# The first batch's token sums of phi as TensorE products with a two-column constant, under a new table of steps

## The chip, the core and the metric

The kernel runs as one launch on one core of a Trainium2 chip. The core's engines are TensorE (matrix products into PSUM), VectorE, ScalarE, GpSimd and SyncE, which here issues the transfers. In the rows they are called PE (with PEld for TensorE's loads of the stationary operand), DVE, ACT, POOL and SP. The metric is the device time of one execution in microseconds (us), taken as the median of a kernel's runs.

## The reference

The inputs are q, k and v of shape 8 x 8 x 576 x 64 (batch, head, token, feature), phi of shape 8 x 8 x 576 x 32, and two weights, 512 x 2048 and 2048 x 512, which arrive as 64-bit floats. The first part is an attention through 32 memories, the second a feed-forward network with a leaky unit.

```
a   = exp(phi - max(phi, axis=tokens))
a   = a / (sum(a, axis=tokens) + 1e-9)
k_m = einsum('bhsm,bhsd->bhmd', a, k)
v_m = einsum('bhsm,bhsd->bhmd', a, v)
scores = (q @ k_m.T) / 8
scores = scores - max(scores)
attn   = exp(scores) / (sum(exp(scores)) + 1e-9)
x = (attn @ v_m), heads side by side           # 4608 x 512
h = x @ w_in                                   # 4608 x 2048
out = maximum(0.01 * h, h) @ w_out             # 4608 x 512
```

The maxima and the sums of phi run over the 576 tokens. Such a sum, for each batch, head and memory, is what the change is about; those over the memories, in the scores' softmax, are not touched.

## The kernel before

**Stages.** The work goes batch by batch. The tokens of all eight heads of a batch are first reduced to the 32 memories: phi lies with 128 rows (two groups g of 64, which is half the heads each) and for each of four heads hh nine slots j of 32 memories (`ld["phi"]`, 128 x 4 x 9 x 32). Step A1 takes maxima over the slots on VectorE (L575), A2 transposes them on TensorE (L589), A3 takes the maximum over rows and builds a diagonal (L596, L599), B0 spreads it back by two products with ones (L605), B1 subtracts and B2 takes the exponential on ScalarE (L614, L620). For the first batch B1 and B2 come in two halves. C1 multiplies the exponentials with k (C10) and v (C11): 72 products of 64 rows, 32 stationary columns and 64 moving columns each, at eight positions of the array (L654), into the two PSUM tiles `pk` of the pool `ps_o`.

**The sums.** B3 adds the exponentials over the nine slots on VectorE (L636 to L639 for the first batch, one reduce at L632 for the others), which leaves sums over slots but not over the 64 rows of each group. C2 transposes these on TensorE into columns 128 to 255 of `pk[0]` (L668), and C30 adds over the 64 rows with a reduce, adds epsilon, takes the reciprocal, and scales it by 1/8 (four operations on VectorE, L677 to L682). C3k and C31 use the reciprocals to form x_k (ScalarE, L689) and x_v (VectorE, L700).

**From there.** D10 and D11 transpose x_k and x_v, D3 and D5 copy the results to SBUF as kT and vT (D6 the low half of vT in later batches). C4, D2 and D4 find a power-of-two scale for the values (L708, L339 and L341, the spread L346, L351). Q0 and Q1 flip the two halves of q on VectorE (L772), E1 computes scores (L793), E2 flips them (L807), and the steps S{chunk}{1 to 8} do the softmax of two chunks: maximum (L827), subtraction (L830), exponential on ScalarE (L835), sum and reciprocal (L839 to L841), scaling (L844), and a flip into the tile `a` (L852 or L857), which is the stationary side of the feed-forward part.

**The weights.** x is never formed: the values of the memories are folded into w_in (W and f steps, products at L909 with vT stationary), so that the first feed-forward product multiplies `a` with the folded weight `w_mem`. The 64-bit weights are loaded in pieces (ld), turned into float32 words by integer operations on ScalarE (L384 and L395) and VectorE (L404; a whole piece is 128 x 768), and later split into a high and a low fp16 half. The first eight units of 96 tokens (u0 to u7; P products at L993, O products at L1061) run in float32, so that they need no split weights; the later ones (p, d and others, L1104 and L1172) in fp16 halves. Bounds on the weights (ci, co, L469 to L487) set the scales of the halves.

**What sets the order.** All of it is cut into named steps, and two strings, `OPENING` and `LATER`, list the steps in the order in which they are emitted. Each engine, and the queue of each engine that issues transfers, runs its own instructions in exactly that order, so the strings are the schedule. `a3.Q0` is step Q0 of batch 3; `z.4` are four idle products of ones with ones, 128 x 512 in float32, which keep TensorE busy (L1260); `f00.1` is the fold of batch 0 with piece 0 of the weight; `p14.2` and `d12.5` are parts of the units 14 and 12.

**Where q is loaded.** The two halves of a batch's q are loaded by SyncE (L566) into the first 12288 bytes of a shared tile `arena`; the tiles of k and v of the same batch (4608 bytes each) lie in part in the same place, so the two transfers of q wait until the products of C10 have read them. The transfer of the next batch's phi (L535) is issued in the same stretch.

## Time and profile before

The median of three runs is 667.87 us (667.07 to 669.79). The profiled execution is another one:

| what | value |
|---|---|
| time of the profiled execution | 668.56 us |
| its span, first to last instruction | 666.0 us |
| TensorE busy | 644.3 us, 97% of the span |
| VectorE busy | 515.2 us, 77% |
| ScalarE busy | 398.6 us, 60% |
| GpSimd busy | 29.8 us, 4% |
| granted TensorE clock, mean over the span | 0.994 of full |
| moved by DMA | 60.37 MB, 91 GB/s in the mean |

A row of a timeline gives the start of an instruction, or of some in a row that are alike, counted from the start of the span, its duration, the engine, the line of the kernel, the operation, the tile written and the tiles read, and their sizes. A bracket at the end is the engine's idle time just ahead of it and what ended that. A float32 product appears as two halves, so `x72` products are 144. A row of the windows gives the busy time of each engine in a stretch, with the granted clock as a share of the full one.

### The profile page before, as it was taken

To read this page: it belongs to the slowest core of one execution; us is meant where nothing else is said; L and a number is where in the kernel's file an instruction comes from. 1 tells how busy PE (TensorE), PEld (TensorE's weight loads), DVE (VectorE), ACT (ScalarE), POOL (GpSimd) and SP (SyncE) were. 2 spreads that over 40 slices of the span, in tenths; PEclk is the share of its full clock that TensorE was granted. 3 is DMA by queue.
4 is the path that set the end of the run, shared out by engine and by line. 5 is a ranking of instruction groups with operands and counts; after the bars stand their busy time and mean duration, and the time that the engine had idled before them with its cause. 6 is when DMAs were issued, how large, how long until landed. Compare 5 with 4: busy or idle time off the path is not lost.

```text
span 666.0 us, 17554 instructions
## 1 busy us (share of the span) xinstructions
PE 644.3 (97%) x7592; PEld 483.1 (73%) x7592; DVE 515.2 (77%) x857; ACT 398.6 (60%) x677; POOL 29.8 (4%) x43
## 2 busy tenths in 40 slices
PE   7799999999999899999998999999999999999997
PEld 3345445665446588888897889898878788989883
DVE  5765869999996699888878885779888887575641
ACT  2789677774663457456644765655665466564543
POOL 0100130000020001000100010000010001000000
PEclk9899999999999899999999999999999999999999
DMA  9989641004602441441051401045103010100101
GB/s 257 400 317 306 239 170 49 1 1 110 188 1 53 103 144 33 109 144 33 10 132 36 142 1 33 5 104 177 33 14 79 15 33 8 27 20 16 33 2 47
DMA packets 32604, 60.37 MB, mean 91 GB/s; under 512 B 4368, under 2 KB 14608, under 8 KB 32528
## 3 DMA queue, kind: packets, MB, share of 16 engines
q1 hardware_dynamic: 32432, 59.13, 29.6%
q8 instruction: 59, 0.97, 0.6%
q10 hardware_dynamic: 96, 0.13, 0.1%
q14 instruction: 17, 0.14, 0.1%
HBM read 49.81 MB, written 9.44 MB: 89 GB/s over the span
## 4 chain that ended last, share of the span: by engine, by line
PE 84%; DMA 8%; DVE 4%; ACT 1%; SPq 1%; issue 1%; DVEq 0%; ACTq 0%
PE po L1172 28%; PE ph L1104 20%; PE po L1061 13%; PE ph L993 8%; PE ph L1172 5%; PE pa L909 4%; DMA arena<-in_q_dram 3%; PE pa L654 2%; PE pa L793 2%; DMA arena<-in_moe_w_in_dram 2%; PE po L1206 1%; DMA wi<-in_v_dram 1%; DMA arena<-in_phi_dram 1%; DMA arena<-in_moe_w_out_dram 1%; DVE arena L772 1%; DVE r1k L575 1%
## 5 line engine op out<-in xcount | busy, mean ns | idle before, releaser
L1172 PEld LDWEIGHTS <-arena 128*128 128x128 f16 x2184 | 209.8, 98 | 32.0 <-issue 9.0
L1120 ACT ACTIVATE wi<-ph,g_sc 128x256 f32<-128x256 f32 (+1 forms) x224 | 99.8, 465 | 167.2 <-PE ph L1104 166.3
L1104 PE MATMUL ph<-a,w_mem 128*128 128x256 f16 (+3 forms) x1440 | 147.1, 247 | 3.3 <-ACT wi L1120 3.1
L1104 PEld LDWEIGHTS <-w_mem 128*128 128x128 f16 x1440 | 115.4, 98 | 18.3 <-issue 6.7
L1172 PE MATMUL po<-wo,arena 128*128 128x256 f16 x936 | 122.5, 273 | 0.0
L1172 PE MATMUL po<-arena 128*128 128x256 f16 x936 | 121.9, 273 | 0.0
L1061 PE MATMUL po<-wo,arena 128*128 128x512 f16 (+1 forms) x384 | 110.7, 434 | 0.0
L1149 DVE TENSOR_TENSOR arena<-arena 128x1024 f16<-128x1024 f32 x52 | 63.2, 1216 | 27.7 <-ACT arena L1145 27.6
L1149 DVE TENSOR_TENSOR arena<-wi,arena 128x768 f16<-128x768 f32 (+1 forms) x60 | 52.9, 882 | 31.5 <-ACT arena L1145 31.3
L1145 ACT CAST arena<-arena 128x1024 f16<-128x1024 f32 x52 | 54.2, 1043 | 10.5 <-DVE arena L1141 10.2
L993 PE MATMUL ph<-a,w_mem 128*128 128x192 f16 (+2 forms) x304 | 53.8, 323 | 1.7 <-DVE a L852 1.7
L1141 DVE TENSOR_TENSOR arena<-wi 128x256 f32<-128x256 f32 x104 | 39.2, 418 | 15.3 <-ACT wi L1120 15.3
L1061 PEld LDWEIGHTS <-arena 128*128 128x128 f16 x288 | 27.8, 98 | 29.3 <-issue 0.9
L1145 ACT CAST arena<-wi 128x768 f16<-128x768 f32 (+1 forms) x60 | 46.5, 775 | 1.8
L1141 DVE TENSOR_TENSOR arena<-wi,arena 128x256 f32<-128x256 f32 x104 | 43.8, 422 | 1.8
L1172 PE MATMUL ph<-wo,arena 128*128 128x256 f16 x312 | 42.6, 273 | 0.0
L876 POOL TENSOR_TENSOR a<-t,a 128x384 f16<-128x384 f32 x22 | 21.4, 997 | 450.9 <-ACT a L871 380.4
L1061 PEld LDWEIGHTS po<-wo,arena 128*128 128x128 f32 x96 | 17.6, 190 | 21.0 <-issue 19.1
L772 DVE STREAM_TRANSPOSE arena<-arena 96x1536 f32<-96x1536 f32 x14 | 24.7, 1766 | 8.0 <-DMA arena<-in_q_dram 3.7
L1000 ACT ACTIVATE arena<-ph,g_sc 128x384 f32<-128x384 f32 x32 | 18.5, 578 | 18.3 <-PE ph L993 17.6
L909 PE MATMUL pa<-wi,vT 64*32 64x512 f16 (+1 forms) x704 | 29.0, 420 | 0.4 <-ACT vT L742 0.4
L993 PEld LDWEIGHTS <-w_mem 128*128 128x128 f16 x240 | 20.8, 98 | 9.3 <-issue 2.7
(204 smaller groups left out, 767.6 us busy)
## 6 DMA issues: line engine op xcount, KB each, us to landing
arena<-in_q_dram SPq DMA_DIRECT2D x16, 576.0 KB, 7.0
out_dram<-obs SPq DMA_DIRECT2D x142, 64.0 KB, 1.7
arena<-in_k_dram SPq DMA_DIRECT2D x28, 288.0 KB, 5.2
arena<-in_v_dram SPq DMA_DIRECT2D x28, 288.0 KB, 5.5
arena<-in_moe_w_in_dram SPq DMA_DIRECT2D x12, 512.0 KB, 7.6
arena<-in_moe_w_out_dram SPq DMA_DIRECT2D x12, 512.0 KB, 6.9
arena<-in_phi_dram SPq DMA_DIRECT2D x7, 576.0 KB, 7.1
arena<-in_moe_w_in_dram SPq DMA_DIRECT2D x8, 256.0 KB, 8.1
```

The source lines that it names most:

```text
L772: nc.vector.transpose(flat, ld["q", g].rearrange("p hh j d -> p (hh j d)"))
L876: nc.gpsimd.tensor_tensor(lo[:, tb], t2[:, tb], hi[:, tb], ALU.subtract)
L909: nc.tensor.matmul(pf[g][cols, :], lhs, rhs, start=(n == 0), stop=(n == len(passes) - 1), tile_position=(g * D, hh * M),)
L993: nc.tensor.matmul(ph[:, t0:t0 + n * SB], lhs, rhs, start=(m == 0), stop=(m == len(seq) - 1))
L1000: nc.scalar.activation(dst, ph, AF.Prelu, scale=sc, alpha=SLOPE)
L1061: nc.tensor.matmul(po, lhs, rhs, start=(f == 0 and m == 0), stop=(f == NQ * NF - 1 and m == len(seq) - 1),)
L1104: nc.tensor.matmul(ph[:, t0:t0 + n], lhs, rhs, start=(m == 0), stop=(m == len(seq) - 1))
L1120: nc.scalar.activation(dst, ph, AF.Prelu, scale=g_sc2[:, j:j + 1], alpha=SLOPE)
L1141: nc.vector.tensor_tensor(gt[:, x], y, z, op)
L1145: nc.scalar.copy(dst[:, 0], src)
L1149: nc.vector.tensor_tensor(dst[:, 1], src, dst[:, 0], ALU.subtract)
L1172: nc.tensor.matmul(acc, g[:, x, s, u], rhs, start=(h == 0 and j == 0 and u == 0 and m == 0), stop=(j == NQ - 1 and u == 1 and m == 2), ski ...
```

## The change

**A constant.** A tile `halves_of_rows` of 128 x 2 in float32 has ones in column 0 for the rows 0 to 63 and in column 1 for the rows 64 to 127 (three fills on GpSimd).

**The sums of the first batch.** Its B3 (four operations on VectorE) and C2 (a transpose) are gone. A new step `a0.C1s` makes 36 products instead, one for each slot and head: stationary is the slot of the exponentials, 128 rows x 32 memories, moving is the constant, two columns. They add up in columns 128 and 129 of `pk[0]`, at four positions of the array, and give the sum over tokens for both groups at once. C30 reads these two columns and loses its reduce. The first product with k into `pk[0]` no longer opens that tile, since the sums do. The later batches compute as before.

**The order.** The whole of `OPENING` and `LATER` is written anew, under the same step names. The number of idle products ahead of the first transpose becomes five in three places, later ones move, and in each of the later phases the transfers come in the order q0, q1, phi of the next batch.

The core of the difference (of `LATER` two places, the stretch of batch 5):

```diff
 OPENING = """
-z.4 a0.phi0 a0.phi1 a0.k a0.q0 a0.A10 a0.A11 a0.A2 a0.q1 a0.A3 a0.B0 z.1 a0.B10 a0.B11 a0.B20
-i0.ld0 a0.B21 a0.C10 a0.B3 i0.ld1 a0.C2 z.1 a0.C30 i0.ld2 a0.Q0 a0.C3k a0.v a0.D10 a0.D3 a0.Q1
-a0.E10 i0.y0 a0.E1 z.3 o0.ld0 i0.h0 a0.E20 i0.y1 a0.E21 i0.t0 o0.ld1 i0.h1 a0.S01 i0.y2 i0.h2
-i0.t1 o0.ld2 a0.S02 o1.ld0 i0.t2 a0.S03 a0.C11 a0.E22 i0.b a0.S11 a0.C31 o1.ld1 a0.S12 a0.D11
-a0.S04 a0.D5 a0.S13 f00.1 o1.ld2 o0.y0 a0.S05 f00.2 i1.ld0 a0.S06 o0.y1 a0.C4 u0.P0 o0.h0
...
+a0.phi0 a0.A10 a0.phi1 a0.A11 a0.k z.3 a0.q0 z.1 z.1 a0.A2 a0.q1 i0.ld0 a0.A3 a0.B0 a0.B10
+a0.B11 a0.B20 a0.B21 i0.ld1 a0.v a0.C1s a0.C10 a0.C30 a0.C3k a0.D10 a0.Q0 a0.D3 i0.y0 i0.ld2
+o0.ld0 a0.Q1 a0.E10 o0.ld1 i0.h0 a0.E1 a0.E22 z.2 a0.E21 i0.y1 a0.S11 i0.h1 i0.t1 i0.y2 a0.E20
+i0.h2 i0.t0 o1.ld0 o0.ld2 a0.S12 a0.C11 a0.S01 a0.S02 a0.S03 i1.ld0 a0.C31 a0.D11 i0.t2 i1.ld1
+a0.D5 i0.b f00.1 f00.2 a0.S04 a0.S05 a0.S13 o0.y0 o1.ld2 a0.S06 z.2 a0.C4 o1.ld1 u0.P0 u0.P1
...
 LATER = """
...
+p15.2 d13.3 v15.2 a5.B20 l14.1 d13.4 p15.3 a5.B3 a5.C10 v15.3 c15.0 l15.0 d13.5 a5.q0 s15 a5.C2
+d13.6 p16.0 a5.C30 p16.1 v16.0 a5.q1 d14.0 a5.C31 v16.1 c15.1 d14.1 a5.C4 a5.D11 a5.C3k d14.2
+l15.1 a6.phi p16.2 a5.Q0 a5.D10 v16.2 a5.D2 a5.D3 d14.3 a5.D4 d14.4 a5.Q1 p16.3 a5.D5 d14.5
...
+    halves_of_rows = const.tile([P, 2], F32, name="halves_of_rows")
+    nc.gpsimd.memset(halves_of_rows, 0.0)
+    for g in range(2):
+        nc.gpsimd.memset(halves_of_rows[g * P // 2:(g + 1) * P // 2, g:g + 1], 1.0)
...
-            n = HP * KJ * M
-            t = wi[3][:, n:n + HP * 4 * M].rearrange("p (hh j m) -> p hh j m", hh=HP, j=4)
-            nc.vector.tensor_tensor(t, ph[:, :, 0:4], ph[:, :, 4:8], ALU.add)
-            nc.vector.tensor_tensor(t[:, :, 0:2], t[:, :, 0:2], t[:, :, 2:4], ALU.add)
-            nc.vector.tensor_tensor(s0, t[:, :, 0], t[:, :, 1], ALU.add)
-            nc.vector.tensor_tensor(s0, s0, ph[:, :, 8], ALU.add)
...
-                            start=(j == 0), stop=(j == KJ - 1), tile_position=(g * D, hh * M),
+                            start=(j == 0 and (b > 0 or kinds == (1,) or g > 0)),
+                            stop=(j == KJ - 1), tile_position=(g * D, hh * M),
+                            skip_group_check=(b == 0),
...
+        def sums_of_phi():
+            var["pk"] = [ps_o.tile([P, E], F32, name="po") for g in range(NG)]
+            for j in range(KJ):
+                for hh in range(HP):
+                    nc.tensor.matmul(
+                        var["pk"][0][hh * M:(hh + 1) * M, P:P + NG], ld["phi"][:, hh, j, :],
+                        halves_of_rows, start=(j == 0), stop=(j == KJ - 1),
+                        tile_position=(0, hh * M), skip_group_check=True,
+                    )
...
+                nc.vector.tensor_scalar_add(r, var["pk"][0][:, P:P + NG], EPS)
```

**TensorE, the start of the program.** Here `ones` and `ident` are constants, `r1k` holds the maxima and then the diagonal, `wi` and `wo` hold k and the exponentials. Before:

```order
L1260 MATMUL pa<-ones 128x512 x4
L589 MATMUL pa<-ident,r1k 128x128
L605 MATMUL pa<-r1k,ones 64x128 x2
L1260 MATMUL pa<-ones 128x512
L654 MATMUL po<-wo_90,wi_86 32x64 x2
```

And with the change:

```order
L1276 MATMUL pa<-ones 128x512 x5
L593 MATMUL pa<-ident,r1k 128x128
L609 MATMUL pa<-r1k,ones 64x128 x2
L665 MATMUL po<-halves_of_rows,wi_90 32x2 x36
L653 MATMUL po<-wo_94,wi_90 32x64 x2
```

A fifth idle product stands ahead of the transpose of the maxima, the one behind the spread is gone, and the 36 sums stand ahead of the products with k.

**VectorE, the softmax of the first chunk.** `t` and `tm` are the scores and their maxima, the operations into `wi` from `arena` are the weight's conversion, `x_v` the scaled values. Before:

```order
L772 STREAM_TRANSPOSE wo_89<-arena 96x1536
L807 STREAM_TRANSPOSE t_308<-pa 128x384 x2
L404 SCALAR_TENSOR_TENSOR wi_84<-arena 128x768
L827 TENSOR_REDUCE tm<-t_308 128x24
L404 SCALAR_TENSOR_TENSOR wi_84<-arena 128x768
L830 TENSOR_TENSOR t_308<-t_308,tm 128x768
L404 SCALAR_TENSOR_TENSOR wi_84<-arena 128x512
L807 STREAM_TRANSPOSE t_308<-pa 128x384
L827 TENSOR_REDUCE tm<-t_308 128x12
L700 TENSOR_SCALAR x_v<-po,r_227 128x64 x2
```

With the change:

```order
L788 STREAM_TRANSPOSE wo_93<-arena 96x1536
L823 STREAM_TRANSPOSE t_338<-pa 128x384 x2
L843 TENSOR_REDUCE tm<-t_338 128x12
L408 SCALAR_TENSOR_TENSOR wi_88<-arena 128x768
L823 STREAM_TRANSPOSE t_338<-pa 128x384
L408 SCALAR_TENSOR_TENSOR wi_88<-arena 128x768
L843 TENSOR_REDUCE tm<-t_338 128x24
L846 TENSOR_TENSOR t_338<-t_338,tm 128x768
L716 TENSOR_SCALAR x_v<-po,r_264 128x64 x2
L408 SCALAR_TENSOR_TENSOR wi_88<-arena 128x512
```

The short chunk's flip and maximum, and the piece that was second among the weight's, now stand ahead of the long chunk's maximum and subtraction; the third piece stands behind them.

**SyncE, the transfers between the k and v of batch 5 and those of batch 6.** Before:

```order
L1039 DMA out_dram<-obs 32x512 x16
L535 DMA arena<-in_phi_dram 128x4x288
L566 DMA arena<-in_q_dram 96x4x384 x2
L546 DMA arena<-in_k_dram 128x576
L546 DMA arena<-in_v_dram 128x576
```

With the change:

```order
L1055 DMA out_dram<-obs 32x512 x8
L570 DMA arena<-in_q_dram 96x4x384 x2
L539 DMA arena<-in_phi_dram 128x4x288
L550 DMA arena<-in_k_dram 128x576
L550 DMA arena<-in_v_dram 128x576
```

The two transfers of q, with q0 the first of them, now go ahead of the next batch's phi.

## Rows read from the trace of the kernel before

**Rows 1.** The page's part 1: busy time of each engine, share, instructions.

```profile
PE 644.3 (97%) x7592; PEld 483.1 (73%) x7592; DVE 515.2 (77%) x857; ACT 398.6 (60%) x677; POOL 29.8 (4%) x43
```

**Rows 2.** Timeline of TensorE, 0 to 40 us: start, duration, operation, tiles, count, [idle].

```profile
6.98 0.27 PE L589 MATMUL pa<-ident,r1k 128*128 128x128 f32 x1
...
10.34 0.37 PE L654 MATMUL po<-wo,wi 64*32 64x64 f32 x10 [0.63 <-ACT wi L620]
...
11.78 0.23 PE L654 MATMUL po<-wi,wi 64*32 64x64 f32 x2
...
29.69 2.76 PE L993 MATMUL ph<-a,w_mem 128*128 128x384 f32 x4 [1.73 <-DVE a L852]
```

**Rows 3.** Timeline of TensorE's weight loads, 6 to 7 us.

```profile
6.12 0.19 PEld L1260 LDWEIGHTS pa<-ones 128*128 128x128 f32 x1 [0.36 <-issue]
6.55 0.14 PEld L589 LDWEIGHTS pa<-ident,r1k 128*128 128x128 f32 x1 [0.24 <-issue]
```

**Rows 4.** Timeline of VectorE, 13 to 30 us.

```profile
13.80 0.17 DVE L682 TENSOR_SCALAR r<-r 128x2 f32<-128x2 f32 x1
...
15.57 1.74 DVE L772 STREAM_TRANSPOSE wo<-arena 96x1536 f32<-96x1536 f32 x1
...
19.40 1.05 DVE L807 STREAM_TRANSPOSE t<-pa 128x384 f32<-128x384 f32 x2 [2.09 <-PE pa L793]
...
21.21 0.94 DVE L827 TENSOR_REDUCE tm<-t 128x24 f32<-128x768 f32 x1
22.07 0.95 DVE L404 SCALAR_TENSOR_TENSOR wi<-arena 128x768 uint32<-128x768 uint32 x1
...
26.04 0.95 DVE L839 TENSOR_REDUCE ts__411<-t 128x24 f32<-128x768 f32 x1
...
28.56 0.98 DVE L852 STREAM_TRANSPOSE a<-t 128x768 f32<-128x768 f32 x1
```

**Rows 5.** Timeline of ScalarE, 20 to 25 us.

```profile
20.49 0.93 ACT L384 ACTIVATE arena<-arena 128x768 uint32<-128x768 uint16 x1
...
23.92 0.84 ACT L835 ACTIVATE t<-t 128x768 f32<-128x768 f32 x1 [1.38 <-DVE t L830]
```

**Rows 6.** Windows: stretch, us, busy PE, PEld, DVE, ACT, POOL, granted clock, DMA, GB/s.

```profile
29.84:33.25 3.41, 3.41 (x7) 1.96 (x8) 2.42 (x8) 2.40 (x5) 1.38 (x1) 0.50 1.03 407
224.40:227.81 3.41, 2.85 (x15) 1.84 (x14) 2.88 (x11) 1.63 (x3) 0.00 (x0) 0.50 0.00 0
100.00:200.00 100.00, 100.00 (x911) 56.16 (x909) 97.15 (x144) 64.21 (x105) 3.94 (x4) 1.00 0.21 58
```

**Rows 7.** Timeline of TensorE, idle marks behind the opening.

```profile
83.62 0.38 PE L487 MATMUL pa<-diag,ones 4*128 4x4 f32 x2 [0.83 <-DVE diag L481]
83.93 2.84 PE L1061 MATMUL po<-wo,arena 128*128 128x512 f32 x6
...
223.46 0.49 PE L346 MATMUL pa<-mdiag,ones 128*128 128x128 f32 x2 [2.15 <-DVE mdiag L341]
...
283.13 0.33 PE L1104 MATMUL ph<-a,w_mem 128*128 128x64 f16 x6 [0.37 <-ACT wi L1120]
...
352.90 0.33 PE L1104 MATMUL ph<-a,arena 128*128 128x128 f16 x3 [1.75 <-ACT wi L1120]
...
521.75 0.81 PE L1104 MATMUL ph<-a,w_mem 128*128 128x256 f16 x6 [1.29 <-ACT wi L1120]
```

**Rows 8.** Timeline of VectorE, flips of q in two of three phases.

```profile
220.88 1.77 DVE L772 STREAM_TRANSPOSE arena<-arena 96x1536 f32<-96x1536 f32 x1 [2.89 <-DMA arena<-in_phi_dram]
...
518.35 1.77 DVE L772 STREAM_TRANSPOSE arena<-arena 96x1536 f32<-96x1536 f32 x1 [1.49 <-DMA arena<-in_q_dram]
```

**Rows 9.** DMA issues of both q, 211 to 214 us: last, us to landing.

```profile
arena<-in_q_dram SPq DMA_DIRECT2D x1, 576.0 KB, 4.9
...
arena<-in_q_dram SPq DMA_DIRECT2D x1, 576.0 KB, 8.4
```

**Rows 10.** The page's part 5: group, count, busy us, mean ns, idle before.

```profile
L1104 PE MATMUL ph<-a,w_mem 128*128 128x256 f16 (+3 forms) x1440 | 147.1, 247 | 3.3 <-ACT wi L1120 3.1
```

## The prediction, made without the result

> **What bounds the kernel now.** I read the engine line of the page first: TensorE is busy for 644.3 of 666.0 us, VectorE for 515.2, ScalarE for 398.6 [rows 1]. So the end is set by the sum of TensorE's work, by the time at which that work starts in earnest, and by every stretch in which TensorE waits. None of the products that make up the bulk is touched by the change; it can win only the 22 us in which TensorE stands, and time at half clock. I then went through TensorE's timeline, row by row, for idle marks.

> They lie in three places. In the opening the first product of the feed-forward part starts at 29.69 us, after 1.73 us of waiting for `a` [rows 2]; from there to 83 us no idle mark follows. In the middle there are a few: 0.83, 2.15, 0.37, 1.75 and 1.29 us are the marks that matter [rows 7]. The rest lies behind the last product, where both orders end alike. [...]

> **The opening.** The chain to 29.69 is: maxima of phi, exponentials, products with k, reciprocal sums, x_k, scores, flips, softmax of chunk 0, L993.

> *The warm-up products.* Before, four stand ahead of the transpose of the maxima (L589), now five. The load of that transpose comes at 6.55 and waited for nothing but the issue [rows 3], and its product starts at 6.98 with no idle mark [rows 2]: the maxima were there, and the warm-ups set its start. A fifth is two more halves, 0.43 us each by the spacing of the last loads (6.12 to 6.55): +0.86 on the chain. The first part of the exponentials then ends not at 10.34 [rows 2] but at 11.2.

> *The sums of phi.* Removed are four adds on VectorE and one transpose (L668); added are 36 float32 products of two columns, ahead of the k products. The trace has no such product. The 72 k products (64 columns, 64 rows) run from 10.34 to 12.01, 23 ns each [rows 2]; by their tile positions eight lie side by side. The new ones fill 128 rows, four side by side, so I take 46 ns: 36 x 46 = 1.66 us. Lower end: 36 x 23 = 0.83 us; nothing at all would change no more, as will be seen. Upper end: the whole-array transpose L589, 0.27 us for its two halves, with nothing side by side: 36 x 0.27 = 9.7 us.

> [...]

> *What the sums gain.* The reciprocal no longer waits for the adds, but the three VectorE operations behind it read the PSUM tile that the k products write too, and in the built program they wait for the last k product. So the sums stand in series with the k products: 11.2 + 1.66 + 1.67 = 14.5, and three operations of 0.20 (0.17 and the gap [rows 4]) give 15.1. Before, the last of the three began at 13.80 and q's second flip ended at 15.57 + 1.74 = 17.31 [rows 4]. The two flips of q (1.74 each, a little of it beside each other) follow directly: 15.1 + 3.4 = 18.5. The second scores wait for that flip, so their end moves from 19.40 [rows 4] by 1.2 to 20.6. The part of the change that gives it its name brings nothing here; the fifth warm-up and the series cost more than the adds did.

> *The softmax of chunk 0.* VectorE has, behind the scores: two flips 1.0, the short maximum 0.5, a weight piece t1, the third flip 0.5, a piece t0, maximum, subtraction. t1 needs ScalarE's second half of piece 1, which ends at 20.49 + 0.93 = 21.42 [rows 5] and hangs on a transfer that is not moved. Long operations follow each other by 0.86 (21.21 to 22.07 [rows 4]). From 22.1: four of them, a flip and the tail of the last: 26.1. The exponential takes 0.84 [rows 5]: 27.0. From there to the end of `a` is 28.56 + 0.98 - 26.04 = 3.5 [rows 4]; 30.5, and the first product at 30.7, +1.0. With the cheap price the chain meets t1 at 21.42 and the product starts at 30.0 (+0.35), also if the sums were free. With the dear one it starts near 38.7 (+9.0). v, asked for one transfer earlier, is no longer awaited in any of these. Late next are the vT copy and the squares, which ScalarE now does behind that exponential.

> *The clock.* Two warm-ups now stand between the fold f00 and the first product, where TensorE idled 1.73 us before the clock fell. I take it that the half-speed stretch at 29.84 goes: 3.41 us, all busy [rows 6], lose 1.7 us of work. Opening in sum: 1.0 - 1.7 = -0.7; ends -1.35 and +7.3. From the first product on, TensorE's queue holds the same work in both orders.

> **The middle.** Of the five waits, three are one mechanism. At 220.88, at 518.35 and once between them (three in all, two shown) VectorE's flip Q0 waits for q, with the spread of the value scale or the activations' halves queued behind it [rows 8]; TensorE's 2.15, 1.75 and 1.29 us follow from them. These are the phases of batches 3, 5 and 7. q can be loaded only after the k and v products have read its place, and in these phases q0 is issued behind q1 (3, 7) or behind the next batch's phi (5). The first of two q transfers lands 4.9 us after its issue, the second 8.4 [rows 9]. In batches 2, 4 and 6 q0 came first, and the wait there is 0.37 [rows 7] or none. The new order asks for q0, q1, phi in every phase. It also has 8 or 9 of TensorE's p and d steps (a p step takes 147.1 us / 224 = 0.65 [rows 10], a d step I set to the same), so 5 to 6 us, between the k products and Q0, and Q0 behind the value scale. So I set the three down to 0.4 each: 5.19 - 1.2 = 4.0. The 0.83 at 83.62 is TensorE waiting for the weight bounds (L481); the new order puts a down product in between, 2.7 us by the one that follows (83.93, to the next step at 86.6) [rows 7]: 0.8. With the 2.15 the second half-speed stretch goes: 2.85 us busy in it [rows 6], 1.4 us.

> Against this I set 1.7 us for new waits: two of the size of the 0.83, since a whole order is replanned and I followed only the phases by hand. From 100 to 200 us VectorE is 97% busy [rows 6], and there the new order puts two long operations more, some 2 us, ahead of the eleventh unit's down products. TensorE has no idle there [rows 6], so there is slack, of a size that no row gives.

> Sum: -0.7 - 4.0 - 0.8 - 1.4 + 1.7 = -5.2 us. The profiled execution took 668.56 us (span 666.0), 0.7 over the median of the runs, 667.87; so 663.4 for that execution and 662.7 for the median.

> **Rivals.**
> *The waits come back elsewhere.* The middle is a new plan, and the order before, planned as a whole too, has 6 us of waits. For it: VectorE's 97%. Against: the named cause, q behind other transfers, is gone in all phases. With all 6 us back and the second half-speed stretch with them, only the opening is left: -0.7, 667.2; with a part, down to 664.5.

> *The opening eats it.* The 36 products at the dear price, +7.3 instead of -0.7: 670.7. For it: four column tiles with a load each for two columns. Against: the k rows.

> *The wait moves from Q0 to Q1 (slower).* Behind Q1 on VectorE stand the low half of vT, which the fold of the next batch needs, and the activations' low halves. Between the k products and that fold stand fourteen p and d steps (9.1 us at 0.65) and small transposes (some 1.0, an estimate): 10.1 us; Q1 and the low half take 2.0. From q1 landing later than 8.1 us, each us is a wait in five phases. The second q took 8.4 with phi close behind [rows 9], which is the 0.4 that I count. At 10.25 us all five stand 2.15: 5 x 2.15 - 6.2 + 1.0 = +5.5, 673; if the clock falls each time as at 223, +1.4 each, 680. Against: in batches 4 and 6, with q0, q1, phi in this order, nothing of the kind shows.

> **How the numbers follow.** Forecast 0.60: 662.7, own range 658.5 to 664.5. Waits elsewhere 0.26: 664.5 to 669. The opening 0.05: 670.7. Q1 0.09: 672 and more. Below 658 only if all waits go and the sums are cheap (-1.35 - 6.0 - 1.4 = 659.1, less the small ones). A range of 658 to 669 leaves out about 2 in 10. A change of 0.5%, 3.3 us, is about what can be told from none: below 664.5 is faster (0.60), to 671.2 the same (0.30), above slower (0.10).

> **What would show it.** Right: the first feed-forward product at 30 to 31 us at full clock; the transpose of the maxima near 7.8; the sums in 0.8 to 1.7 us, and the reciprocal behind the last k product; no wait of Q0 for q; one half-speed stretch less at 224. Wrong: a first product later than 33, idle marks over 1 us in batches 3, 5 or 7, or a new half-speed stretch.

## The result, and the profile after

The changed kernel takes 668.77 us (median of 20 runs, 667.06 to 671.81) where the kernel before, run beside it, takes 667.06 (20 runs, 663.23 to 671.29): a ratio of 1.0032, 95% interval 1.0018 to 1.0046. It is slower, by 0.3%, where 0.8% faster was forecast (662.7 against 667.87). The profiled execution took 671.58 us, 2.8 over its median, with a span of 669.7; that of before took 668.56, 1.5 over its median, with a span of 666.0. So the two executions read here lie 3.0 us apart in time and 3.7 in span, the medians 1.7. The 3.7 us are two large parts of opposite sign.

The page's busy times after [rows 1]: the work on TensorE has hardly grown.

```profile
PE 647.5 (97%) x7663; PEld 486.0 (73%) x7663; DVE 520.9 (78%) x852; ACT 397.7 (59%) x677; POOL 33.3 (5%) x46
```

The timeline of TensorE after, 0 to 42 us (columns as in [rows 2]):

```profile
7.64 0.27 PE L593 MATMUL pa<-ident,r1k 128*128 128x128 f32 x1
...
11.05 0.91 PE L665 MATMUL po<-halves_of_rows,wi 128*32 128x2 f32 x72 [1.73 <-issue]
...
17.96 0.32 PE L653 MATMUL po<-wo,wi 64*32 64x64 f32 x3 [4.11 <-issue]
...
32.34 0.27 PE L653 MATMUL po<-wi,wi 64*32 64x64 f32 x2 [1.56 <-issue]
...
35.70 3.78 PE L1276 MATMUL pa<-ones 128*128 128x512 f32 x4
39.27 2.96 PE L1009 MATMUL ph<-a,w_mem 128*128 128x384 f32 x8
```

The sums are cheap: 72 halves in 0.91 us. But among the products with k, which before ran without a gap, TensorE stands still for 4.11 us, and again for 1.56 among those with v, which stand ahead of the fold. The view names no engine, semaphore or transfer for either ("issue"). The first feed-forward product comes at 39.27 instead of 29.69, so 9.6 us later.

VectorE after, where the reciprocal starts and where `a` is done:

```profile
18.45 0.16 DVE L696 TENSOR_SCALAR r<-po 128x2 f32<-128x2 f32 x1 [7.67 <-PE po L653]
...
35.96 0.98 DVE L868 STREAM_TRANSPOSE a<-t 128x768 f32<-128x768 f32 x1
```

With [rows 4] these divide the 9.6 us. The reciprocal's last step ends at 19.02 instead of 13.97, +5.05, of which 4.11 are the stop. From there to the end of `a` it takes 17.92 instead of 15.57, +2.35. `a` is ready at 36.94, but two idle products, which stand behind the delayed fold, hold TensorE until 39.27: +2.2. The order of VectorE's operations, the stop of 1.56 us ahead of the fold and the clock all bear on the last two parts, and this trace alone doesn't part them. The windows after (columns as in [rows 6]) show two stretches at a granted clock of 0.50 in the opening, where before had the one of 3.41 us; the first begins at 12.40, ahead of the long stop:

```profile
12.40:29.47 17.07, 10.43 (x250) 5.88 (x244) 8.63 (x13) 5.59 (x9) 1.44 (x2) 0.50 1.03 391
32.88:39.71 6.83, 6.37 (x22) 2.25 (x23) 5.27 (x11) 5.23 (x8) 0.00 (x0) 0.50 0.52 182
```

From the first feed-forward product to the end, the kernel before takes 636.3 us (666.0 - 29.69), the changed one 630.4: here it wins 5.9. The windows of the middle after:

```profile
80.00:100.00 20.00, 18.29 (x158) 9.10 (x156) 14.15 (x36) 14.05 (x24) 4.01 (x4) 1.00 0.57 203
100.00:200.00 100.00, 98.26 (x867) 54.40 (x867) 93.22 (x145) 65.59 (x108) 10.09 (x9) 1.00 0.28 82
200.00:300.00 100.00, 99.44 (x1335) 75.34 (x1334) 88.01 (x144) 54.27 (x96) 3.20 (x4) 1.00 0.28 74
300.00:400.00 100.00, 100.00 (x1377) 86.71 (x1375) 90.75 (x144) 61.96 (x108) 4.02 (x5) 1.00 0.29 83
```

TensorE idles 4.5 us from 80 to 600 (0.45 of it between 500 and 600) where the same windows of before add up to 8.1. The waits of 2.15, 1.75 and 1.29 us [rows 7] are gone, and no flip of q waits for a transfer [rows 8]:

```profile
L788 DVE STREAM_TRANSPOSE arena<-arena x14: 1732/1767/1774, 75.2 to 517.6; 96x1536 f32<-96x1536 f32 x14
...
its engine sat idle before it (us, times) until:
  PE pa L653: 1.6, 1
```

In place of the 0.83 at the weight bounds there is a new wait of 1.71, of the scores of batch 1 for kT:

```profile
87.05 1.26 PE L809 MATMUL pa<-arena,kT 32*32 32x192 f32 x57 [1.71 <-ACT kT L752]
```

### The profile page after: what moved, and what is told of

Same layout as the page of the kernel before. It is cut to its first block, busy times and chain, and to the rows that moved or that the text cites. A ratio compares the mean times of both kernels' runs of the same rounds, so it can differ in the third digit from the quotient of the medians.

```text
span 669.7 us, 17690 instructions
## 1 busy us (share of the span) xinstructions
PE 647.5 (97%) x7663; PEld 486.0 (73%) x7663; DVE 520.9 (78%) x852; ACT 397.7 (59%) x677; POOL 33.3 (5%) x46
## 3 DMA queue, kind: packets, MB, share of 16 engines
q1 hardware_dynamic: 32432, 59.13, 29.8%
## 4 chain that ended last, share of the span: by engine, by line
PE 93%; DVE 3%; issue 1%; DMA 1%; ACT 1%; SPq 0%; POOL 0%; ACTq 0%; DVEq 0%; POOLq 0%
PE po L1188 31%; PE ph L1120 21%; PE po L1077 13%; PE ph L1009 7%; PE ph L1188 5%; PE pa L925 4%; PE pa L809 2%; PE pa L653 2%; PE pa L1276 2%; PE po L1222 1%; DMA arena<-in_moe_w_in_dram 1%; PE po L653 1%; DVE wo L423 1%; PE pa L735 1%; PE pa L609 1%
## 5 line engine op out<-in xcount | busy, mean ns | idle before, releaser
L1120 PE MATMUL ph<-a,w_mem 128*128 128x256 f16 (+3 forms) x1440 | 145.5, 246 | 1.0 <-ACT wi L1136 1.0
L1165 DVE TENSOR_TENSOR arena<-arena 128x1024 f16<-128x1024 f32 x52 | 63.8, 1227 | 34.0 <-ACT arena L1161 33.8
L1009 PE MATMUL ph<-a,w_mem 128*128 128x192 f16 (+2 forms) x304 | 52.4, 317 | 0.1
L1077 PEld LDWEIGHTS <-arena 128*128 128x128 f16 x288 | 27.6, 98 | 31.3 <-issue 1.0
L1157 DVE TENSOR_TENSOR arena<-wi,arena 128x256 f32<-128x256 f32 x104 | 47.2, 453 | 1.8
L892 POOL TENSOR_TENSOR a<-t,a 128x384 f16<-128x384 f32 x22 | 23.9, 1109 | 437.9 <-ACT a L887 383.6
L1157 DVE TENSOR_TENSOR arena<-wi 128x256 f32<-128x256 f32 x104 | 40.6, 433 | 0.2
L1016 ACT ACTIVATE arena<-ph,g_sc 128x384 f32<-128x384 f32 x32 | 18.6, 581 | 25.1 <-PE ph L1009 23.8
L954 DVE SCALAR_TENSOR_TENSOR w_mem<-pa,w_mem 128x512 f16<-128x512 f32 x40 | 26.0, 681 | 2.0 <-ACT w_mem L948 1.9
```

Source lines behind the costliest of these rows:

```text
L892: nc.gpsimd.tensor_tensor(lo[:, tb], t2[:, tb], hi[:, tb], ALU.subtract)
L954: nc.vector.scalar_tensor_tensor(t[:, 1], src["w"][g] if b else w32[j][g], ws, t[:, 0], ALU.mult, ALU.subtract)
L1009: nc.tensor.matmul(ph[:, t0:t0 + n * SB], lhs, rhs, start=(m == 0), stop=(m == len(seq) - 1))
L1077: nc.tensor.matmul(po, lhs, rhs, start=(f == 0 and m == 0), stop=(f == NQ * NF - 1 and m == len(seq) - 1),)
L1120: nc.tensor.matmul(ph[:, t0:t0 + n], lhs, rhs, start=(m == 0), stop=(m == len(seq) - 1))
L1157: nc.vector.tensor_tensor(gt[:, x], y, z, op)
```

## What the stops have in common

I counted TensorE's records in the trace from the start of the program: its loads, its products' halves and the semaphore instructions of its sequencer, which the timeline leaves out, together. To one record, the stop of 4.11 us stands in front of the 450th, the one of 1.56 us in front of the 962nd, and a third of 0.85 at 148 us in front of the 2754th: 450, 450 + 2 x 256, 450 + 9 x 256. I call such a place a border. In the kernel before the only stop without a releaser, 0.43 us, is in front of the 450th too, but there that record lies in the scores:

```profile
18.31 0.92 PE L793 MATMUL pa<-wo,kT 32*32 32x192 f32 x38 [0.43 <-issue]
```

The DMA view has a queue of its own for instructions; in the stop, from 15 to 17 us, it shows one packet among the loads (kind, packets, MB, share):

```profile
q1 hardware_dynamic: 277, 0.77, 99.7%
q8 instruction: 1, 0.02, 3.3%
```

That packet starts at 15.56 and ends at 16.61, TensorE goes on at 17.96. The page counts 60 such packets of 0.98 MB in all, so 16 KB each, and the records have 59 borders. So the theory, inferred from these numbers and shown by no view, was: a packet brings the 256 records that follow a border; those behind the 450th record arrive at some 18 us; the 36 sums are 144 records (72 halves and 72 loads), and they moved that border from the scores, which waited for kT and q anyway, into the products with k, on which everything else in the opening waits. The rivals were the new opening order, the clock, and late transfers.

## The experiments

Each ran in five rounds beside the kernel before; e9 and e13, which are not in the table, ran once. "First product" is the first feed-forward product, "stop" the one in front of the 450th record.

| run | median us (runs) | ratio to before, 95% | span of profile | first product | stop |
|---|---|---|---|---|---|
| change | 668.77 (20) | 1.0018 to 1.0046 | 669.7 | 39.27 | 4.11 |
| e1 opening of before | 664.11 (8) | 0.9936 to 0.9972 | 659.8 | 28.45 | under 0.3 |
| e2 later order of before | 675.22 (6) | 1.0102 to 1.0146 | 674.6 | 39.29 | 5.00 |
| e3 before + 36 unused sums | 678.73 (5) | 1.0161 to 1.0208 | 678.1 | 38.04 | 5.04 |
| e4 nine wide sums | 664.79 (12) | 0.9951 to 0.9977 | 662.3 | 33.84 | 0.45 |
| e5 before + 28 unused sums | 676.22 (6) | 1.0107 to 1.0163 | 674.1 | 34.73 | 3.30 |
| e6 e1 + idle products | 663.47 (7) | 0.9918 to 0.9967 | 659.7 | 29.35 | under 0.3 |
| e7 sums on VectorE | 663.87 (8) | 0.9934 to 0.9970 | 661.5 | 31.33 | under 0.3 |
| e8 e4 + idle products | 664.12 (9) | 0.9929 to 0.9966 | 663.3 | 33.27 | 1.43 |
| e10 e7 + idle products | 664.04 (12) | 0.9944 to 0.9977 | 660.5 | 29.82 | under 0.3 |
| e11 change + idle product | 669.63 (12) | 1.0028 to 1.0067 | 667.2 | 37.45 | 5.66 |
| e12 before, q order alone | 663.51 (12) | 0.9939 to 0.9980 | 660.2 | 29.07 | 0.15 |
| e14 idle products cut small | 667.48 (12) | 0.9992 to 1.0025 | 665.7 | 36.76 | 4.70 |
| e15 40 products ahead | 667.75 (12) | 0.9987 to 1.0030 | 665.1 | 36.15 | 3.36 |

### The two halves of the change: e1 and e2

e1 has `OPENING` and the sums of before with the new `LATER`, e2 the reverse:

```diff
 run(OPENING.split())   # e1: of before   e2: of the change
 run(LATER.split())     # e1: of the change   e2: of before
```

> The opening of before (sums on VectorE, a transpose) with the new order behind it. Theory (the loss sits in the opening alone: TensorE gets the instructions behind its 450th record only at some 18 us, and the 36 sums have brought that record into the products with k): first feed-forward product at 29.7 us as before, waits of the middle gone as in the changed kernel; 636.3 us behind that product become 630.4 plus 1.7 for the half-clock stretch at 29.8, so about 663 us (662 to 664) against 667.1 of before. Rival (the middle gains only because it starts 10 us later and its transfers have landed by then): the waits for q come back, 665 to 668.

> The changed opening with the old order behind it. Theory: first feed-forward product near 39 us as in the changed kernel, the middle's waits as before: 667.1 + some 6 = 673 us (671 to 675). Rival (the two parts interact, as above): the old middle has its waits covered by the later start too, 669 to 670.

The loss lies in the opening, the gain behind it: e1 is 0.46% faster than before, e2 1.2% slower. From the first product to the end of the span the new order wins 4.9 us behind either opening (631.4 against 636.3, and 630.4 against 635.3). These are single executions, off their medians by +1.5 (before), -2.0 (e1), +2.8 (the change) and +1.2 us (e2). By the medians the new order wins 2.8 us behind the old opening and 6.5 behind the new one, and both runs come out just above their ranges. Why the two differ is not settled; e2's stop of 5.00 us is longer than the change's, and e2 has a further stop without a releaser of 1.32 us at 451 us.

### The sums put into the kernel before: e3 and e5

```diff
-i0.ld0 a0.B21 a0.C10 a0.B3 i0.ld1 a0.C2 z.1 a0.C30 i0.ld2 a0.Q0 a0.C3k a0.v a0.D10 a0.D3 a0.Q1
+i0.ld0 a0.B21 a0.C1s a0.C10 a0.B3 i0.ld1 a0.C2 z.1 a0.C30 i0.ld2 a0.Q0 a0.C3k a0.v a0.D10 a0.D3 a0.Q1
```

In e5 the added step runs over seven slots instead of nine.

> The kernel before, in its own order, with the 36 two-column products in front of those with k, their result unused. Theory (instruction supply): TensorE stops inside the products with k at its 450th record, for 3 us or more, until 17.5 to 18.5 us; the first feed-forward product moves from 29.7 to 34 or later, and the time to 672 us or more. Rival 1 (the sums cost only what they take, 0.9 us, and the loss comes from the new order of the opening): 668 us, the stop stays inside the scores. Rival 2 (the long stop is a late transfer that the new order moved): 668 as well.

> The kernel before with 28 unused sums instead of 36: 112 more records of TensorE, so its 450th falls on the transposes of x_k, behind the products with k (which end at the 435th). Theory (a block of instructions that arrives at some 18 us, wherever TensorE stands): the wait no longer lies in front of the reciprocal, x_k and its transposes, so all that was ready by 16 us before is ready again; the first feed-forward product at 30 to 32.5 us against 38 with 36 sums, 667 to 670 us. Rival (each added record costs its share): 28/36 of the 11.9 us, 675 to 677.

e3 does nothing but add 0.9 us of work whose result nobody reads, and costs 11.9 us. Its chain of waits (start, duration, what):

```profile
10.60 0.91 PE po L669 x69
11.51 1.46 PE po L658 x94
12.97 5.04 issue
18.01 0.44 PE po L658 x9
```

Order, idle products and transfers are those of before: rivals 1 and 2 are out. Only 8.4 us of the loss lie ahead of the first product (38.04 against 29.69). The added records move every later border too, and three of these now fall among products with k and v, where the kernel before has no such stop:

```profile
77.85 0.41 PE L658 MATMUL pa<-arena 64*32 64x128 f32 x11 [1.12 <-issue]
...
278.82 0.44 PE L658 MATMUL pa<-arena 64*32 64x128 f32 x14 [0.95 <-issue]
...
454.75 0.41 PE L658 MATMUL pa<-arena 64*32 64x128 f32 x4 [1.44 <-issue]
```

They add up to 3.5 us, nearly the 3.8 by which e3's span behind the first product is longer than that of before. e5 is a miss in the time, 676.22, where the rival (each record costs its share) said 675 to 677. Its chain shows why:

```profile
14.97 1.67 DVE wo L788
16.64 1.26 issue
17.90 2.78 PE pa L809 x93
...
28.84 1.06 PE pa L925 x9
29.91 2.22 issue
32.12 1.99 PE pa L925 x7
```

The first border behaved as the theory said: the reciprocal is early, q is flipped by 16.64, and the stop costs 1.26 on the chain. But the second, the 962nd record, now falls in the fold ahead of the first feed-forward product, whose block isn't there until 32.12; before, TensorE reached it at 44.7. I had counted one border only, and behind the first product there are two stops more, of 0.97 and 1.04 us. The rival's figure is met by another mechanism than its own.

### Other ways to the sums, and the clock: e4, e7, e8, e10

e4 makes the constant the stationary side, nine products of 128 columns into two rows, which are copied and transposed. e7 has the changed order with the sums on VectorE. e8 and e10 add one idle product behind the spread and one behind the transposed sums.

```diff
-                for hh in range(HP):
-                    nc.tensor.matmul(
-                        var["pk"][0][hh * M:(hh + 1) * M, P:P + NG], ld["phi"][:, hh, j, :],
-                        halves_of_rows, start=(j == 0), stop=(j == KJ - 1),
-                        tile_position=(0, hh * M), skip_group_check=True,
-                    )
+                nc.tensor.matmul(
+                    var["ps"][:NG], halves_of_rows, ld["phi"][:, :, j, :],
+                    start=(j == 0), stop=(j == KJ - 1),
+                )
```

> The changed kernel, but the sums as nine products of 128 columns with the constant as the stationary side, a copy and a transpose of two columns: 20 TensorE operations' halves instead of 72, 104 records fewer, the same sums. Theory (instruction supply): the 450th record lies in the scores, no stop of over 1 us inside the products with k, first feed-forward product at 31 to 34 us instead of 39.3 (the higher end if the clock still falls at 12 us), 661 to 665 us. Rival (the order of the opening and its missing idle products, not the count): 668 to 669 as with the change.

> The changed kernel's whole order, but the sums on VectorE with the transpose as before (no two-column products). It separates the sums from the new opening order. Theory: no stop inside the products with k, the 450th record lies in the scores; what is left is the order's own cost, the missing idle products and half clock: first feed-forward product at 31 to 35 us, 663 to 667 us. Rival (the new opening order is the loss): 668 to 670, first feed-forward product at 37 us or later.

> As e4_swapped (nine products of 128 columns for the sums), with one idle product behind the spread and one behind the transposed sums, where the order before had them. If TensorE's idle stretch of 1.7 us at 9 us brought the half clock from 11.3 us on: full clock up to the scores, sums in 1.6 instead of 3.3 us, first feed-forward product at 30 to 32 us instead of 33.8, 662 to 663.5 us. Rival (the clock falls all the same at the next wait): 664 to 665.

> As e7_dve_sums (new order, sums on VectorE), with one idle product behind the spread and one behind the transposed sums. e7 ran its opening at half clock from 11.5 to 25.1 us. If TensorE's idle stretch at 9 us is what brought the clock down: full clock to 20 us or longer, first feed-forward product at 29 to 30 us instead of 31.3, 662 to 663 us against 663.9. Rival (the clock falls anyway, or the time is set elsewhere): 663.5 to 664.5.

With 106 or 142 records fewer the stop leaves the products with k, and the changed order is worth 664.79 and 663.87: it wasn't the order. In e4 the nine wide sums took 3.27 us (2.13 in e8), far more than the 36 narrow ones' 0.91, and it is faster all the same. The clock gave nothing that shows, and for e8 and e10 the rivals' figures came. e10 ran at full clock throughout (granted 1.000 in the mean) and started its first product 1.5 us earlier than e7, yet the medians are the same, 664.04 and 663.87; the earlier TensorE met a stop of 1.37 us in front of the 706th record, which e7 has not. In e8 the clock held to 20 us, but the stop grew from 0.45 to 1.43, since TensorE came 1.4 us sooner to a block whose packet came 0.2 sooner.

### Idle products alone: e6 and e11

```diff
-f00.1 ... a0.C4 u0.P0 o0.h0          # e6, from e1
+f00.1 ... a0.C4 z.2 u0.P0 o0.h0
-a0.A3 a0.B0 a0.B10                   # e11, from the change
+a0.A3 a0.B0 z.1 a0.B10
```

> The old opening with the new order behind it, and two idle products in front of the first feed-forward product, where TensorE waited 1.6 us. This tests the prediction's clock term by itself. If the fall of the clock at 29 us comes from that wait: granted clock 1.0 throughout the opening, 1.7 us of work not lost, less up to 0.4 for the end of the idle products: 662.5 to 663.2 against 664.1. Rival (the fall comes from what stands earlier, or the idle products come late and delay the first product): 664 to 665.

> The changed kernel with one idle product more, behind the spread (four records). It parts the changed opening's loss into the stop for instructions and the half clock. Theory: the stop at the 450th record stays (3 to 5 us among the products with k), the clock falls only behind it, so the first feed-forward product at 36 to 38.5 us instead of 39.3, 666 to 668.5 us. Rival (the clock, fallen at 12.4 us, is the loss): first feed-forward product at 33 or earlier, 664.

e6 does keep the full clock (0.999 in the mean), and its first product comes 0.9 us later behind the idle ones. Its median is 0.6 lower than e1's, with ranges that lie over each other; the 1.7 us of the prediction's clock term are not shown. e11 holds the clock 3 us longer, to 15.52, and still loses, with a median above its range: the stop is 5.66, since TensorE reaches the border earlier and goes on at 18.94. Here the clock falls inside the stop; in the changed kernel it fell at 12.40, ahead of it and behind the 1.73 us without work. Moving the fall back did not bring the loss down, and e7, without the stop, runs at half clock from 11.5 to 25.1 us and wins: the fall at 12.40 is not what makes the loss.

### Why the block is late: e9 and e13

```diff
-                nc.sync.dma_start(st[:, x - c0:x - c0 + m], src[:, x // FQ, x % FQ:x % FQ + m])
+                nc.scalar.dma_start(st[:, x - c0:x - c0 + m], src[:, x // FQ, x % FQ:x % FQ + m])
...
-a0.B21 i0.ld1 a0.v a0.C1s a0.C10 a0.C30 a0.C3k a0.D10
+a0.B21 a0.C1s a0.C10 a0.C30 a0.C3k a0.q0 a0.q1 a0.v a0.D10   # e13; e9 keeps q and v
```

> The changed kernel, but the loads of the weights are issued by ScalarE behind the copy of kT instead of by SyncE from 4.7 us on, so that from some 9 us to the scores only k, q and v are on the DMA engines. It asks why the block behind TensorE's 450th record comes at 18 us. If the instruction packet is late because the DMA engines are full: TensorE passes its 450th record with a stop under 1.5 us instead of 4.4, and the first instruction packet starts before 14.5 us. Rival (the block comes at a fixed time, or at a fixed distance behind an earlier record): a stop of 3 us or more, the packet at 15 to 16 us. The total is longer in both, since the weights come late, and is not read.

> As e9_late_weights, and the loads of q and v too are issued by ScalarE only behind x_k, so that the DMA engines carry nothing but phi and k before it. If full DMA engines make the instruction packet late: it starts within 2 us of TensorE's 66th record instead of 5, and the stop at the 450th record is under 1.5 us instead of 4.4. Rival (the way takes this long by itself): packet 4.4 us or more behind the 66th record, stop 3 us or more. The total, which is much longer since all loads come late, is not read.

e9 told nothing: its stop was 4.55 us, with the loads of q and v still ahead of x_k. In e13 these too come behind it, and the packet starts at 11.92, 0.55 us behind TensorE's 194th record instead of 3.6. The stop on the timeline:

```profile
14.36 0.32 PE L653 MATMUL po<-wo,wi 64*32 64x64 f32 x3 [0.86 <-issue]
```

0.86 instead of 4.11 us, with TensorE's instructions in the same order: it is the loads of the opening that make the block late. In what way they do, by filling the engines or by standing ahead in a queue, is not shown. (The totals, 688.5 and 692.2 us, come from the late loads.)

### What asks for the block: e14 and e15

```diff
-                pi, ones, ones.unsqueeze(1).broadcast_to([P, NF, P]), start=True, stop=True
+            for x in range(NF):
+                nc.tensor.matmul(pi[:, x], ones, ones, start=True, stop=True)   # e14
...
-a0.phi0 a0.A10 a0.phi1 a0.A11 a0.k z.3
+a0.phi0 a0.A10 a0.phi1 a0.A11 a0.k t. z.3   # e15: t. is 40 products of two columns
```

> The changed kernel, but the five idle products at the start are cut into twenty of 128 columns: the same columns, 60 records more. TensorE then passes its 66th record at some 4.5 us instead of 10.9. Theory (the block is asked for when an early record is passed): the first packet starts near 10 us instead of 15.6, the block is there by 13 us, the stop among the products with k is under 1.5 us, first feed-forward product at 33 to 36 us instead of 39.3, 663 to 667 us. Rival (the packet comes at its time, and 60 more records only use up the budget): stop of 5 us or more, among the first products with k, 670 us or more.

> The changed kernel with 40 more two-column products of ones, unused, at the very start, ahead of the five idle products: 160 records more, some 0.6 us, after which TensorE passes its 194th record at 5 to 6 us instead of 12. Theory (the first block is asked for when TensorE passes a record between the 94th and the 194th, and comes 6 to 7.5 us later while the loads run): first packet at 8 to 11 us, no stop over 1 us among the products with k although 160 more records stand ahead of them; the next block's stop then falls on the 706th record, in the scores, until 18.5 to 21 us; first feed-forward product at 31 to 36 us instead of 39.3, 662 to 667 us. Rival (the packet comes at 15 to 16 us whatever TensorE has passed): a stop of 5 us or more at the 450th record, now ahead of or early in the products with k, 672 us or more.

Neither number came. In e14 the 66th record is passed 4 us earlier, the packet is not (16.23): it is not that record which asks. In e15 the packet is 1.2 us earlier than with the change (14.36), and the stop is shorter, 3.36, although 160 records more stand ahead; its rival is out. I had placed the 194th record too early: it was passed at 9.6, not at 5 to 6. In all executions with loads the packet starts 3.5 to 4.8 us behind the 194th record; which one asks for it stays open. Against one up to the 94th speak e14 and e15, which pass that one 1.5 and 9.7 us earlier than the change, without a packet to match; in e13 the packet starts as the 271st is passed. Both medians are 1 us lower than the change's, with intervals that overlap its own. That was not expected. In both profiles the 962nd record is passed without a stop, the second stretch at half clock is missing, and the first product comes 2.5 and 3.1 us earlier, in e14 behind a longer first stop.

### The order of q alone: e12

```diff
-a3.q1 a3.q0 a4.phi
+a3.q0 a3.q1 a4.phi
...
-a6.phi
-a5.q0 a5.q1
+a5.q0
+a5.q1 a6.phi
...
-a7.q1 a7.q0
+a7.q0 a7.q1
```

> The kernel before, with one change: in the phases of batches 3, 5 and 7 the transfers are issued in the order q0, q1, phi. It tests the prediction's step on the middle by itself. By that step TensorE's waits of 2.15, 1.75 and 1.29 us fall to some 0.4 each and the second half-clock stretch goes: 5.4 us, so 661.5 to 663.5 us. Rival (q1 then is late for Q1 instead, or the new order's longer way between the products with k and Q0 is what hides q): 665 to 667, with waits behind Q1 or Q0 still there.

663.51, at the upper end of the 661.5 to 663.5 that the prediction's step gives: 3.3 us won of the 5.4. TensorE's waits for the activation's halves in the view of waits (engine, line, waited for: us, times, longest), which in the kernel before were 5.3, 7 and 1.8:

```profile
PE ph L1104 <- ACT wi L1120: 3.7, 6, 1.1
```

The flips of q wait for no transfer any more, the waits of 2.15 and 1.29 are gone, the one of 1.75 is 1.05, and the second half-clock stretch is gone. Three places in the table are worth as much, within the intervals, as the whole replanned `LATER` in e1 (0.9939 to 0.9980 against 0.9936 to 0.9972).

## Why the prediction was wrong

**The fifth idle product:** +0.86 forecast, +0.66 measured (7.64 against 6.98). Right, a little too large.

**The price of the sums:** 1.66 us forecast between 0.83 and 9.7; measured 0.91, 12.6 ns a half, near the lower end. That the reciprocal waits for the last product with k was right (7.67 us of waiting, released by L653).

**The first feed-forward product, +1.0 us: the step that failed.** It came 9.6 us later. I bounded what the new products cost while they run, 0.83 to 9.7 us, and the chain from there on waits only for data: the sum has no term for an instruction that has not arrived. What the products cost was room: 144 records ahead of a border at which TensorE waits for instructions, here 4.11 us and then 1.56. e3 shows it in the kernel before, e4 and e7 show the stop gone with the records, e13 shows that loads set the size. The rival "the opening eats it" gave a total near the truth, 670.7, for a reason that is false here. The 0.43 without a releaser stood in the trace of before, and I had passed over it.

**The clock, -1.7:** the stretch at 29.84 did not go, it became 23.9 us at half speed (granted 0.50) in two stretches. The profiled execution has the lowest granted clock of the twenty (0.981, others up to 0.987), so not each has both. And the term was too large by itself: kept at full clock, e6 and e10 gained nothing that shows.

**The middle:** -4.0 for q, -1.4 for the second stretch at half clock, -0.8, +1.7 for new waits, and the -1.7 of the stretch at 29.84, in sum -6.2; from the first product on 5.9 were won. The mechanism of q holds by e12, at 3.3 us in the median. The 0.83 was a miss: a wait of 1.71 came in its place. The 1.7 for new waits had no named cause; what came were that 1.71 and the stop of 0.85 us at 148 us. So the near sum is in part luck.

The range, 658 to 669, held the median of 668.77 by luck: its upper part stood for waits that come back in the middle, and those did not. The sign was wrong.

## What to carry to other kernels

Count the instructions that stand ahead of the first long product, not only their time: a float32 product here is four records, and 36 products that take 0.9 us cost 11.9 in e3: 8.4 where a block of instructions has to come while the loads of the opening run, and some 3.5 where later borders were moved among short products. Look for idle marks for which the profile names no releaser, at a fixed count of instructions, before adding small products: here they were that border in 39 of 46 cases. Where a replanned order brings a gain, try its smallest part first: three places of the table gave as much as the plan.

## What the runs showed of the hardware

```profile
272.12 0.41 PE L654 MATMUL pa<-arena 64*32 64x128 f32 x4 [1.45 <-issue]
```

It lies in the products with k and v of a later batch, short and many like those of the opening, as most of the late ones do. The kernel before and e12 have no such stop of 0.7 us anywhere; the new order has two late ones in e1, e6, e7 and e10, some 2.3 to 3 us, which would be the next to take away.
